# A fused attention and feed-forward kernel: its opening of 879 tasks in another order on all engines

## The chip, the cores and the metric

The kernel runs on one core of a Trainium2 chip. The metric is the device time of one execution in microseconds; the time before is the median of three runs. TensorE (PE) does matrix products, VectorE (DVE) and ScalarE (ACT) elementwise work and reductions, GpSimd (POOL) some elementwise work and DMA issues, and SyncE (SP) issues most DMAs. Each engine works through its own queue in order and waits for the others by semaphores.

## The reference

q, k and v have the shape (8 batches, 8 heads, 576 tokens, 64). The output of an attention with two parts goes through a gated feed-forward network:

```python
q_d, k_d, v_d = [t.reshape(B, H, 144, 4, D).mean(axis=3) for t in (q, k, v)]
out_d = softmax(q_d @ k_d.T / 8) @ v_d                       # coarse, per head
out_up = np.repeat(out_d, 4, axis=2)
mask = np.abs(pos[:, None] - pos[None, :]) < 4               # local, 7 keys a token
out_local = softmax(where(mask, q @ k.T / 8, -1e9)) @ v
x = (out_up + out_local).transpose(0, 2, 1, 3).reshape(4608, 512)
xn = x / sqrt(mean(x * x) + 1e-6) * rms_g
g, val = xn @ w_gate, xn @ w_val                             # 512 -> 1536
out = (g * sigmoid(g) * val) @ w_out                         # 1536 -> 512
```

## The kernel before

The 4608 tokens are cut into 18 chunks of 256. For each chunk the local attention gives x, x is normed and turned so that the features lie on the partitions, and the feed-forward part follows. x, the weights and the hidden values are each kept as a high and a low half (line 1051 and 1055 for x, 1435 and 1438 for the hidden values), and each product is done in three steps, high by high, high by low and low by high. `first` (line 1412) is a group of 12 products for one of 12 slices of the hidden layer, either gate or value; `second` (line 1453) is a group of six for the second layer.

The coarse attention (class `Coarse`) goes by batch and pair of heads: scores (line 589), maxima, powers, turns of the powers on TensorE (line 619), values (line 634). Its results go to DRAM and are read back by the chunks that add them. The local attention of most chunks (class `Attention`) runs on VectorE and ScalarE, with 7 keys for a token (lines 931, 935, 977, 984, 994). Chunks 0 and 1 (class `Early`, two units each) do it on TensorE instead (lines 1180, 1182 for scores, 1241 and 1252 for turns, 1272 for values, 1279 to add the coarse part, 1317 to turn x).

The weights arrive as 64-bit numbers in 20 pieces and are decoded (`decode`): a load on SP's queue, a scaling on ScalarE (line 267), the last bits on GpSimd (line 277), a join on VectorE (line 284), the high half on ScalarE (line 291) and the low half on VectorE, called a split (lines 296 and 298). Raw pieces share a few places, so a later load waits until an earlier piece has been split. The first four pieces are what the first `first` of chunk 0 needs.

All work from the start to the end of chunk 2's feed-forward part, with the local attention of chunks 2 and 3 and the coarse attention of batches 0 to 2, is written as 879 tasks. A task has an engine (or two to choose from: a negative number n in the order stands for task ~n on its second engine), a function that issues its instructions, tasks that must come before it, and buffers that it takes or uses. `ORDER` is a list of all tasks; `plan.run` issues them in that order. The order thus sets each engine's queue, and a wait for a semaphore is put in wherever a task needs another's result or buffer. The first `HELD` tasks are issued under a manual schedule, which keeps their order; those behind may be moved by the framework's scheduler, as may the rest of the kernel, which loops over chunks 3 to 17.

Task numbers that are named below: 0 and 37 load q and k of batch 0 (two halves), 1 and 38 v; 2 to 4 add up the first half, 5 and 42 reorder q; 549 loads the first weight piece, 555, 561, 567 the next three, 550 and 551 take the first one's last bits and scale it; 82 to 88 are the first scores of unit 0; 150 is the low half of chunk 0's second unit, 669 the first `first` of chunk 0, 733 and 734 its last `second` groups, 739 the first `first` of chunk 1, 451 the turn of chunk 2's x, 809 the first `first` of chunk 2, 874 its last `second`.

`run` before also keeps a small model of the engines: costs in microseconds per task, a delay from engine to engine, a DMA rate. From it `heat` (line 416) gets the idle time that TensorE would have ahead of a task, and fills 95% of that with products of a constant with zeros (line 457, called idle products here): 512 or fewer columns each, into a spare tile or into the tile that the next product will overwrite.

Of the kernel before, what the change touches and what calls it, by code (L numbers as in the profile page):

```python
# [19 lines left out]
P = 128  # L20
# [6 lines left out]
SP = S + 2 * HALO  # L27
# [22 lines left out]
HOP = {"PE": 0.25, "ACT": 0.2, "DVE": 0.15, "POOL": 0.2, "SP": 0.0}  # L50
WARM_AT = 6.5
COLD_UNTIL = 15.0
WARM_SHARE = 0.95
WARM_LEAST = 0.4
MB = 3.1
LAND = 2.0
# [44 lines left out]
]  # L101
HELD = 813


class Buf:
# [16 lines left out]
class Plan:  # L122
# [19 lines left out]
    def room(self, t):  # L142

        at, taken = 0.0, {}
        for b in t.allocs:
# [3 lines left out]
            if i >= len(order):  # L149
                return None  # L150
# [1564 lines left out]
```

## Time and profile before

| | us |
|---|---|
| median of 3 runs | 1088.38 (1087.9 to 1089.17) |
| the profiled execution | 1087.48 |
| its span, first to last instruction | 1085.7 |
| TensorE busy | 1062.6 (98%) |
| VectorE busy | 915.3 (84%) |
| ScalarE busy | 596.8 (55%) |
| GpSimd busy | 161.0 (15%) |

The execution is the span and what lies around it, 1.8 us. Busy time counts every instruction of an engine, the idle products too. The mean granted clock of TensorE over the span is 0.994 of full speed; 1 is 2.4 GHz and 0.5 is 1.2 GHz.

### The profile page before, as it was taken

Reading aid. Unit: us, or ns where it says so; the run is one execution under the profiler, and the core shown is the slowest. Engines: PE = TensorE matmul, PEld = TensorE weight load, DVE = VectorE, ACT = ScalarE, POOL = GpSimd, SP = SyncE. Lnnn points to the kernel's source line nnn. Section 1 sums busy time; section 2 is a strip of 40 time slices with the busy share of each in tenths; the row PEclk is TensorE's granted clock in tenths of the full one; section 3 lists DMA queues with packets and bytes.
Section 4 is the critical chain, followed back from the end, with each engine's and each line's share of the span. In section 5 each row is a group of like instructions: output and inputs, shape, how many; then the busy total and the mean of one; then the engine's idle time right before and its main releaser. Section 6 shows DMA issues by size and latency. Waiting matters only on the chain.

```text
span 1085.7 us, 21681 instructions
## 1 busy us (share of the span) xinstructions
PE 1062.6 (98%) x8013; PEld 964.6 (89%) x8013; DVE 915.3 (84%) x1556; ACT 596.8 (55%) x2029; POOL 161.0 (15%) x200
## 2 busy tenths in 40 slices
PE   7899999999999999999999999999999999999998
PEld 4668899998988999999999999999999989899997
DVE  7889899798969998989898989898989898985322
ACT  5775566647356556565555656464746464554111
POOL 5364454401110000000000000000000000000000
PEclk9899999999999999999999999999999999999999
DMA  9966557422644454444444443443222231300000
GB/s 292 326 168 190 143 126 167 99 78 73 149 95 108 99 127 104 123 83 113 91 103 109 102 112 95 116 98 85 72 76 72 74 87 56 104 16 20 1 21 20
DMA packets 78126, 113.83 MB, mean 105 GB/s; under 512 B 31966, under 2 KB 39334, under 8 KB 78020
## 3 DMA queue, kind: packets, MB, share of 16 engines
q1 hardware_dynamic: 48116, 88.11, 26.7%
q0 software_dynamic: 11680, 19.81, 11.9%
q10 hardware_dynamic: 18224, 4.53, 1.9%
q8 instruction: 63, 1.03, 0.4%
q14 instruction: 43, 0.35, 0.1%
HBM read 100.86 MB, written 11.53 MB: 104 GB/s over the span
## 4 chain that ended last, share of the span: by engine, by line
PE 74%; DVE 5%; ACT 2%; DMA 2%; issue 1%; POOL 1%; ACTq 0%; DVEq 0%; SPq 0%; POOLq 0%
PE ps_h L1412 45%; PE ps_o L1453 23%; PE ps_a L634 2%; ACT prod L977 1%; DVE x_t L994 1%; PE ps_a L589 1%; PE ps_a L619 1%; PE ps_a L1047 1%; DMA qk<-in_qk_sum_dram 1%; DVE prod L931 1%; DMA vs<-in_v_sum_dram 1%; DVE prod L984 1%; DVE sc L935 0%; DVE hs L1438 0%; DMA kv<-in_k_pad_dram 0%
## 5 line engine op out<-in xcount | busy, mean ns | idle before, releaser
L1412 PE MATMUL ps_h<-xh,w 128*128 128x256 f32 x3456 | 620.0, 279 | 0.0
L1412 PEld LDWEIGHTS ps_h<-xh,w 128*128 128x128 f32 x3456 | 532.3, 188 | 8.5 <-issue 4.5
L1412 PE MATMUL ps_h<-xl,w 128*128 128x256 f32 x1728 | 479.6, 278 | 0.0
L1453 PE MATMUL ps_o<-wo,hs 128*128 128x512 f32 x1296 | 328.8, 396 | 4.8 <-DVE hs L1438 3.7
L1412 PEld LDWEIGHTS ps_h<-xl,w 128*128 128x128 f32 x1728 | 324.9, 188 | 4.4 <-issue 0.6
L977 ACT ACTIVATE prod<-kv,sc 128x64 f32<-128x64 f32 x1024 | 263.2, 409 | 26.5 <-DVE sc L968 9.2
L1453 PEld LDWEIGHTS ps_o<-wo,hs 128*128 128x128 f32 x1296 | 231.8, 188 | 49.6 <-DVE hs L1438 6.3
L1435 ACT ACTIVATE hs<-sil 128x512 fp32r<-128x512 f32 x108 | 68.4, 633 | 173.9 <-DVE sil L1429 136.1
L931 DVE TENSOR_TENSOR prod<-q_t,kv 128x896 f32<-128x896 f32 x128 | 137.1, 1093 | 3.5 <-DMA q_t<-in_q_band_dram 2.9
L994 DVE TENSOR_REDUCE x_t<-prod 128x128 f32<-128x896 f32 x128 | 134.5, 1076 | 3.2 <-ACT prod L977 3.1
L935 DVE TENSOR_REDUCE sc<-prod 128x14 f32<-128x896 f32 x128 | 135.1, 1076 | 0.2
L1420 ACT ACTIVATE sil<-ps_h 128x512 f32<-128x512 f32 x108 | 64.5, 598 | 128.0 <-PE ps_h L1412 116.7
L1424 DVE SCALAR_TENSOR_TENSOR sil<-sil,ps_h 128x512 f32<-128x512 f32 x108 | 73.7, 683 | 52.7 <-ACT sil L1420 52.0
L984 DVE TENSOR_TENSOR prod<-sc,kv 128x384 f32<-128x384 f32 (+1 forms) x128 | 105.6, 862 | 0.2
L1429 DVE SCALAR_TENSOR_TENSOR sil<-sil,ps_h 128x512 f32<-128x512 f32 x108 | 74.0, 686 | 35.6 <-PE ps_h L1412 35.5
L1438 DVE TENSOR_TENSOR hs<-sil,hs 128x512 fp32r<-128x512 f32 x102 | 71.2, 698 | 19.4 <-ACT hs L1435 19.1
L369 POOL DMA_DIRECT2D qk<-in_qk_sum_dram x42 | 38.8, 923 | 231.6 <-DMA qk<-in_qk_sum_dram 187.9
L369 POOL DMA_DIRECT2D vs<-in_v_sum_dram x42 | 37.2, 886 | 235.1 <-DMA vs<-in_v_sum_dram 158.4
L609 ACT ACTIVATE a_g<-ps_a,m_g 72x144 f32<-72x144 f32 x128 | 46.6, 373 | 33.7 <-DVE m_g L604 21.3
L634 PEld LDWEIGHTS ps_a<-vs,a_g 72*72 72x72 f32 x512 | 39.1, 148 | 8.6 <-DVE a_g L709 3.6
L1017 ACT ACTIVATE up_t<-x_t 128x128 f32<-128x128 f32 x128 | 39.4, 308 | 10.7 <-DVE x_t L1007 8.8
L634 PE MATMUL ps_a<-vs,a_g 72*72 72x64 f32 x512 | 40.1, 232 | 4.2 <-DVE a_g L709 3.4
(155 smaller groups left out, 805.5 us busy)
## 6 DMA issues: line engine op xcount, KB each, us to landing
kv<-in_k_pad_dram SPq DMA_DIRECT2D x56, 320.0 KB
kv<-in_v_pad_dram SPq DMA_DIRECT2D x56, 320.0 KB
qk<-in_qk_sum_dram POOLq DMA_DIRECT2D x42, 288.0 KB, 4.6
out_dram<-o_sb SPq DMA_DIRECT2D x92, 72.0 KB
vs<-in_v_sum_dram POOLq DMA_DIRECT2D x42, 144.0 KB, 3.8
q_t<-in_q_band_dram SPq DMA_DIRECT2D x150, 36.0 KB
w<-in_w_gate_dram SPq DMA_DIRECT2D x8, 512.0 KB
w<-in_w_val_dram SPq DMA_DIRECT2D x8, 512.0 KB
```

Source lines behind the costliest of these rows:

```text
L369: nc.gpsimd.dma_start(out=t, in_=(qk_sum, v_sum)[i][self.b, j, :, self.half], accum_op=ALU.add)
L634: in_line(lambda: nc.tensor.matmul(out=op[:, par, c], lhsT=at[:, kc, c * HALF:(c + 1) * HALF], rhs=self.sums.vs[:, 2 * (self.hp % 2) + par ...
L931: nc.vector.tensor_tensor(out=pr, in0=bcast(q[:, s0:s0 + 2], 2, NO), in1=window(k, s0), op=ALU.mult)
L935: nc.vector.tensor_reduce(out=self.sc[:, j, par, s0:s0 + 2], in_=self.pr[i], axis=AX.X, op=ALU.add,)
L977: nc.scalar.activation(out=self.pr[i][:, o, s], in_=self.v[j, par][:, s0 + s + o], func=AF.Copy, scale=p[:, s, o:o + 1],)
L984: (nc.vector if engine == "DVE" else nc.gpsimd).tensor_tensor(out=self.pr[i][:, a:b], in0=bcast(p[:, :, a:b].rearrange("p s o -> p o s"), ...
L994: nc.vector.tensor_reduce(out=self.x[j][:, s0:s0 + 2, par], in_=pr.rearrange("p o s d -> p s d o"), axis=AX.X, op=ALU.add,)
L1412: self.last = nc.tensor.matmul(out=p[n][:, i], lhsT=wi[:, k], rhs=xi[:, k], start=(m == 0), stop=(m == 3 * KT - 1),).ins
L1424: nc.vector.scalar_tensor_tensor(out=self.sil[n], in0=self.sil[n], scalar=1.0, in1=self.g[n], op0=ALU.add, op1=ALU.mult,)
L1429: nc.vector.scalar_tensor_tensor(out=self.sil[n], in0=self.sil[n], scalar=0.5, in1=self.v[n], op0=ALU.mult, op1=ALU.mult,)
L1438: low["last"] = (nc.gpsimd if engine == "POOL" else nc.vector).tensor_tensor(out=self.hs[n][:, 1], in0=self.sil[n], in1=self.hs[n][:, 0], ...
L1453: in_line(lambda: nc.tensor.matmul(out=self.o[j], lhsT=lhs[:, j * P:(j + 1) * P], rhs=rhs, start=(f == 0 and m == 0), stop=(f == NF - 1 an ...
```

## The change

The 879 tasks stand in another order. The first 850 of them, in place of 813, keep it; the last 29 may be moved by the scheduler. The small model of the engines is gone: `run` only checks that what a task needs has been issued. Idle products are now written down by task, in `IDLE`: 26 of 512 columns, ahead of six tasks (46 and 82, 86, 113, 158, 174: scores and a turn), in place of 135. Some tasks change engines: VectorE has 305 of the tasks in place of 310, ScalarE 224 in place of 222, GpSimd 90 in place of 87. The tasks themselves, and the code behind the opening, are the same. The diff, with all but the first rows of the two orders left out:

```diff
-HOP = {"PE": 0.25, "ACT": 0.2, "DVE": 0.15, "POOL": 0.2, "SP": 0.0}
-WARM_AT = 6.5
-COLD_UNTIL = 15.0
-WARM_SHARE = 0.95
-WARM_LEAST = 0.4
 MB = 3.1
-LAND = 2.0
 ISSUE = 0.75
 ORDER = [
-    151, 0, 37, 182, 76, 75, 77, 78, 549, 5, 2, 3, 4, 1, 153, 82, -185, 9, 83, 84, 42, 39, 555, 11, 10, 12, 40,
-    14, 41, 13, 17, 550, 38, 85, 18, 15, 551, 90, 23, 19, -17, 92, 110, 552, 152, 91, 567, -7, 79, 86, -8, 88,
...
+    77, 549, 551, 75, 0, 2, 79, 5, 3, 4, 110, 37, 82, 182, 76, -185, 78, 9, 10, 11, 83, 1, 555, 84, 85, 90, 42,
+    39, 550, 91, 12, 552, -7, 86, 87, 14, -8, 13, 92, 17, 18, 151, 88, 23, 89, 24, 15, 573, 93, 25, 26, 94, 28,
...
 ]
-HELD = 813
+HELD = 850
+IDLE = {46: 2, 82: 10, 86: 6, 113: 4, 158: 1, 174: 3}
...
     def run(self, order):
 
-        free = self.free
         for n in order:
             t = self.tasks[max(n, ~n)]
-            e, cost, _ = t.options[n < 0]
-            at = self.room(t)
-            assert at is not None and all(a.end is not None for a in (*t.after, *t.with_)), n
-            known = max(free[e], at)
-            s = max([known, t.not_before, free["DMA"] - 3.0 if t.dma else 0.0] + [a.end for a in t.after] + [a.start + 0.01 for a in t.with_])
-            t.start = self.now = s
-            self.idle, self.gap = (s - max(known, WARM_AT), s - max(free[e], WARM_AT)) if e == "PE" else (0.0, 0.0)
-            free[e] = s + cost
...
-            t.engine = e
+            assert self.room(t) and all(a.done for a in (*t.after, *t.with_)), n
+            t.done = True
             for b in t.allocs:
                 self.order[b.res].append(b)
-            t.fn(e) if len(t.options) > 1 else t.fn()
+            self.now = t.n
+            t.engine = t.options[n < 0][0]
+            t.fn(t.engine) if len(t.options) > 1 else t.fn()
...
     def heat(out, fresh=True):
 
-        n = plan.idle
+        n = IDLE.get(plan.now, 0)
+        if not n:
+            return
         if spare["open"] and made:
             if "tile" not in spare:
                 spare["tile"] = ps_o.tile([P, DM], FP32, name="ps_o")
-            out, fresh, n = spare["tile"], True, plan.gap
-        n, plan.idle, plan.gap = n * WARM_SHARE, 0.0, 0.0
+            out, fresh = spare["tile"], True
...
-        rate = 1200 if plan.now < COLD_UNTIL else 2400
-        for _ in range(int(n * rate / cols) if n > WARM_LEAST and made else 0):
+        for _ in range(n * 4 * P // cols):
```

## Rows read from the trace of the kernel before

**Rows 1.** Windows by stage: us, busy us (instructions), granted clock, DMA share, GB/s.

```profile
6.60:76.40 69.80, 61.63 (x373) 40.38 (x374) 61.28 (x111) 50.37 (x139) 37.01 (x40) 0.93 0.87 277
76.40:166.20 89.80, 89.80 (x694) 79.53 (x693) 83.87 (x127) 53.94 (x129) 46.15 (x56) 1.00 0.61 153
166.20:258.20 92.00, 91.86 (x661) 84.33 (x660) 77.92 (x133) 50.59 (x185) 24.59 (x37) 1.00 0.44 98
258.20:400.00 141.80, 139.23 (x1105) 127.62 (x1104) 128.08 (x221) 84.97 (x329) 17.31 (x20) 1.00 0.49 113
400.00:800.00 400.00, 400.00 (x3147) 372.80 (x3147) 364.83 (x639) 228.89 (x833) 31.77 (x37) 1.00 0.42 102
```

The engines in each row are PE, PE's weight loads, DVE, ACT and POOL.

**Rows 2.** Windows of line 457 alone, the idle products: PE, PE's weight loads.

```profile
0.00:76.40 76.40, 20.53 (x72) 7.38 (x72) 0.93 0.85 274
...
98.00:128.00 30.00, 10.79 (x58) 5.64 (x58) 1.00 0.74 192
...
258.00:400.00 142.00, 0.71 (x5) 0.55 (x5) 1.00 0.49 113
```

**Rows 3.** Timeline of PE: start us, us, line, out<-in, count.

```profile
76.42 0.47 PE L1412 MATMUL ps_h<-xh,w 128*128 128x256 f32 x1
...
98.26 4.94 PE L457 MATMUL ps_o<-zero_sb,one_sb 128*128 128x512 bf16 x22
102.84 1.74 PE L1453 MATMUL ps_o<-wo,hs 128*128 128x512 f32 x6
```

**Rows 4.** Timelines of DVE, ACT and POOL, 6 to 13 us: [idle before <-releaser].

```profile
6.66 0.76 DVE L425 TENSOR_TENSOR qk<-w 128x576 f32<-128x576 f32 x1 [0.79 <-DMA w<-in_qk_sum_dram]
...
6.66 1.99 ACT L419 COPY hs<-w 128x1024 f32<-128x1024 f32 x1 [3.45 <-DMA w<-in_qk_sum_dram]
9.73 2.00 ACT L419 COPY hs<-w 128x1024 f32<-128x1024 f32 x1 [1.08 <-DMA w<-in_qk_sum_dram]
...
12.82 1.10 POOL L277 TENSOR_SCALAR w<-w 128x1024 uint32<-128x1024 uint16 x1 [3.70 <-DMA w<-in_w_val_dram]
```

**Rows 5.** Groups of DVE's instructions, 6.6 to 76.4 us: busy us, mean ns, idle before.

```profile
L284 DVE SCALAR_TENSOR_TENSOR w<-w 128x1024 uint32<-128x1024 uint32 x8 | 10.0, 1249 | 0.5 <-ACT w L267 0.5
L1195 DVE TENSOR_REDUCE m_e<-ps_h 128x2 f32<-128x272 f32 x16 | 6.8, 430 | 3.5 <-PE ps_h L1182 3.5
...
L433 DVE TENSOR_TENSOR vs<-vs,w 72x512 f32<-72x512 f32 x3 | 2.9, 962 | 0.9 <-POOL vs L433 0.8
L1165 DVE TENSOR_TENSOR kv<-kv,side_sb 64x512 f32<-64x512 f32 x2 | 2.3, 1136 | 0.0
...
L709 DVE COPY a_g<-ps_a 72x288 f32<-72x288 f32 x2 | 0.9, 438 | 0.1
L709 DVE COPY prod<-ps_a 128x512 f32<-128x512 f32 x1 | 0.7, 692 | 0.1
...
L1307 DVE TENSOR_SCALAR x_t<-x_t,rinv 128x512 f32<-128x512 f32 x1 | 0.5, 486 | 0.0
```

**Rows 6.** Windows around PE's longest wait, columns as in the first group.

```profile
32.00:36.00 4.00, 0.60 (x6) 0.60 (x7) 3.97 (x6) 3.13 (x8) 1.49 (x3) 0.95 1.00 342
36.00:42.00 6.00, 6.00 (x34) 4.63 (x33) 5.44 (x8) 3.98 (x9) 2.98 (x3) 0.50 0.82 239
```

**Rows 7.** Timeline of PE around the same wait.

```profile
30.53 0.76 PE L1182 MATMUL ps_h<-w,hs 64*128 64x136 f32 x4
...
35.40 1.11 PE L634 MATMUL ps_a<-vs,a_g 72*72 72x64 f32 x8 [3.44 <-DVE a_g L709]
...
36.67 1.27 PE L1182 MATMUL ps_h<-w,hs 64*128 64x136 f32 x4
```

**Rows 8.** Windows by stage, behind the opening, columns as in the first group.

```profile
320.00:340.00 20.00, 18.34 (x144) 17.02 (x143) 18.84 (x27) 17.54 (x68) 4.20 (x5) 1.00 0.58 121
340.00:360.00 20.00, 19.52 (x140) 17.58 (x139) 20.00 (x29) 5.51 (x20) 0.00 (x0) 1.00 0.29 82
```

More of the change, by code (lines that the diff above doesn't have):

```diff
@@ L112, with __init__ @@
 class Task:
-    def __init__(self, n, options, fn, due, after, with_, allocs, uses, not_before, dma, lag):
-        self.n, self.options, self.fn, self.due = n, options, fn, due
-        self.after, self.with_, self.allocs = after, with_, allocs
-        self.not_before, self.dma, self.lag = not_before, dma, lag
-        self.start = self.end = None
+    def __init__(self, n, options, fn, after, with_, allocs, uses, dma, lag, not_before):
+        self.n, self.options, self.fn, self.after, self.with_, self.allocs = n, options, fn, after, with_, allocs
+        self.dma, self.lag, self.not_before, self.done = dma, lag, not_before, False
         for b in (*allocs, *uses):
@@ L125, in __init__ @@
     def __init__(self, bufs):
-        self.tasks, self.bufs, self.idle, self.now = [], bufs, 0.0, 0.0
-        self.free = {e: 0.0 for e in ("PE", "ACT", "DVE", "POOL", "SP", "DMA")}
+        self.tasks, self.bufs, self.now = [], bufs, None
         self.order = {r: [] for r in bufs}
@@ L135, in add @@
         t = Task(
-            len(self.tasks), options, fn, due, [a for a in after if a], [a for a in with_ if a],
-            [*allocs, *[Buf("hw") for _ in range(hw)], *[Buf("sw") for _ in range(sw)]], list(uses), not_before, dma, lag,
+            len(self.tasks), options, fn, [a for a in after if a], [a for a in with_ if a],
+            [*allocs, *[Buf("hw") for _ in range(hw)], *[Buf("sw") for _ in range(sw)]], list(uses), dma, lag, not_before,
         )
@@ L142, in room @@
     def room(self, t):
-        at, taken = 0.0, {}
+        taken = {}
         for b in t.allocs:
@@ L148, in room @@
             taken[b.res] = taken.get(b.res, 0) + 1
-            if i >= len(order):
-                return None
-            if i >= 0:
-                for u in order[i].users:
-                    if u.end is None:
-                        return None
-                    at = max(at, u.end)
-        return at
+            if i >= len(order) or i >= 0 and not all(u.done for u in order[i].users if u is not t):
+                return False
+        return True
     def run(self, order):
-        free = self.free
         for n in order:
             t = self.tasks[max(n, ~n)]
-            e, cost, _ = t.options[n < 0]
-            at = self.room(t)
-            assert at is not None and all(a.end is not None for a in (*t.after, *t.with_)), n
-            known = max(free[e], at)
-            s = max([known, t.not_before, free["DMA"] - 3.0 if t.dma else 0.0] + [a.end for a in t.after] + [a.start + 0.01 for a in t.with_])
-            t.start = self.now = s
-            self.idle, self.gap = (s - max(known, WARM_AT), s - max(free[e], WARM_AT)) if e == "PE" else (0.0, 0.0)
-            free[e] = s + cost
-            if t.dma:
-                free["DMA"] = max(free["DMA"], s + cost) + t.dma
-                t.end = free["DMA"] + LAND
-            else:
-                t.end = s + cost + (t.lag or HOP[e])
-            t.engine = e
+            assert self.room(t) and all(a.done for a in (*t.after, *t.with_)), n
+            t.done = True
             for b in t.allocs:
                 self.order[b.res].append(b)
-            t.fn(e) if len(t.options) > 1 else t.fn()
+            self.now = t.n
+            t.engine = t.options[n < 0][0]
+            t.fn(t.engine) if len(t.options) > 1 else t.fn()
 @with_exitstack
@@ L1594, in attn_moe_kernel @@
     plan.run(ORDER[HELD:])
+    plan.now = None
     att, late, behind = atts[FIRST], [], None
```

78 rows, old and new, of the table ORDER are left out of this document.

## The prediction

> **What bounds the kernel now.** I read the busy time by stage first. From 76.4 us on TensorE is busy in every stage, fully so from 400 to 800 us, where VectorE has 364.83 of 400 us [rows 1]. What TensorE gets done earlier in the opening therefore reaches the end of the run, as long as VectorE keeps up. The opening's loss is hidden in the word busy: the idle products of line 457 are counted as TensorE work. Windows of that line alone show 20.53 us of them before 76.4 us and 10.79 us between 98 and 128 us [rows 2]. They are waits written as work. TensorE's timeline shows both kinds of place: the first product of the feed-forward part at 76.42 us, and 22 idle products from 98.26 to 102.84 us while the first second-layer product waits for its hidden values [rows 3]. Ahead of the first feed-forward product VectorE has 61.28 us of work in 69.80 us, and between 76.4 and 166.2 us 83.87 in 89.80 [rows 1]. So VectorE sets the pace of the opening up to about 166 us, with 8.5 and 5.9 us of idle time of its own, and TensorE sets it afterwards (VectorE 77.92 of 92.00 us, TensorE 91.86).
>
> Three sums decide the change: what stands in VectorE's queue ahead of the first feed-forward product, how VectorE's and TensorE's queues keep pace behind it, and what is left of TensorE's idle time between 258 and 400 us.
>
> **Part 1: up to the first feed-forward product.** Its last condition is the low half of the first chunk's x (the split of unit 1, task 150) and the four decoded pieces of W1 (tasks 554, 560, 566, 572). I list VectorE's tasks ahead of task 150 in both orders: 95 before, 86 after, the same but for twelve that leave and three that enter. Leaving: four joins of weight bits that are needed only later (606, 600, 594, 624), 4 x 1.25; one placing of edges that goes to GpSimd (81), 1.14; two copies of 72x288 (16, 32), 2 x 0.44; one copy of 128x512 (134), 0.69; one norm (143), 0.49; two maxima (190, 192), 2 x 0.43; one tiny scaling that I leave out. That is 9.1 us by the means of these lines [rows 5]. Entering: a 128x512 copy (100), 0.69; an addition of v (45), 0.96; a copy of an edge (105), which I bound by the 72x288 copy at 0.44. That is 2.1 us. VectorE's queue ahead of task 150 gets 7.0 us shorter. TensorE's own queue ahead of task 669 holds the same 50 tasks.
>
> Against this stands the load order. SP's queue begins with 0, 37, 549 before, and with 549, 0, 37 after. The three land at 6.66, 9.73 and 12.82 us: the first addition and the first reordering copy wait for the first, the second copy for the second, the last-bits step for the third [rows 4]. So a weight piece takes 12.82 - 9.73 = 3.1 us of the queue, and in the new order the q and k sums land 3.1 us later. VectorE's first addition moves from 6.66 to about 9.8 us, and until then VectorE has only the masks to build. ScalarE's first task becomes the scaling of that piece, which is over before the q sums land, so it costs nothing there.
>
> VectorE's remaining idle time of 8.5 us is what no row of before prices in the new order. Below, it falls to about 4 us when the first two units' scores, softmax and turns follow each other as closely as the order puts them; above, it grows by 3 us because TensorE, without idle products to bring it to the higher clock, does its small products later. I take it as unchanged. Part 1 then gives 7.0 - 3.1 = 3.9 us: task 669 at about 72.5 us.
>
> The idle products themselves cost nothing before 72 us in either order, and so give nothing: before, they lie in time in which TensorE waits for VectorE and ScalarE (the wait is still 3.44 us long at 35.40 us [rows 7]); after, 26 of them remain, 10 ahead of the first score and 6 ahead of the third, both of which wait for q anyway.
>
> **Part 2: behind it, to the end of the opening.** All six places that keep idle products (tasks 46, 82, 86, 113, 158, 174) come before task 669. From there to task 874 the new order has none, where before has 10.79 us of them [rows 2] and 0.14 us of idle time [rows 1]. Real TensorE work is the same. How long TensorE waits now follows from VectorE. From task 669 to the second-layer product 733, which needs the last decoded pieces of W2, TensorE's new queue has 31 groups of 12 first-layer products, 10 groups of second-layer products and 20 small ones: 69.8 us by their durations in the trace. VectorE's queue from behind task 150 to the split 662 has 91 tasks, among them 13 joins, 13 splits, 17 score steps of the local attention and 16 gates, products and low halves: 70.7 us. So both engines are full. With VectorE's busy share of the like stretch before, 83.87 / 89.80 = 93% [rows 1], its 70.7 us take 75.7, and TensorE waits 5.9 us. A second point is the turn of chunk 2's x (task 451): TensorE 110.9 us, VectorE 148 tasks and 110.8 us, 118.6 at 93%, so 7.7 us. Bounds: 1 us if VectorE is never idle, 10.9 us (nothing gained) if the waits return in full. I take 7. Part 2 gives 10.9 - 7 = 3.9 us.
>
> **Part 3: behind the opening.** Between 258.2 and 400 us TensorE is idle for 141.80 - 139.23 = 2.6 us and runs 0.71 us of idle products [rows 1, 2]; VectorE is busy for 38.84 of the 40 us from 320 to 360 [rows 8]. Before, tasks from the 814th on could slip behind other work; now only the last 29 can, and all products of the third batch's coarse attention stand ahead of task 874, so its results, which chunk 4 adds, are ready earlier. The gain lies between 0 and 3.3 us; I take 1.1.
>
> The sum is 3.9 + 3.9 + 1.1 = 8.9 us. The profiled execution took 1087.48 us (span 1085.7 and 1.8 around it) and would take 1078.6. The median of the three runs lies 0.9 above it, so I predict 1088.38 - 8.9 = 1079.5 us. The bounds are 0.9 to 8.4 for part 1, 0 to 9.9 for part 2 and 0 to 3.3 for part 3. Their ends seldom meet; the half-widths of 3.8, 5 and 1.7, added as squares, give 6.5, and the forecast's own range is 1073 to 1086.
>
> **Rivals.**
>
> *The clock falls: slower.* TensorE's granted clock went to 0.50 (the 1.2 GHz level) from 36 to 42 us, right behind its idle stretch of 3.44 us, in a window of 32 to 36 us in which it was busy for 0.60 [rows 6, 7]. At that level four score products took 1.27 us instead of 0.76 [rows 7], 1.67 times. With 26 idle products in place of 72 ahead of task 669, TensorE has longer gaps. Its real work between 6.6 and 76.4 us is 61.63 - 20.53 = 41.1 us [rows 1, 2]; at the lower level throughout that would be 68.6, start at 11.8 us (q lands at 9.8, its reordering takes 2.0 [rows 4]) and end no earlier than 80 us, with some of today's waits at about 85. Part 1 turns from 3.9 gained to 8.6 lost, and the run ends at 1092. TensorE's free time in the new opening is 72.5 - 11.8 - 41.1 - 5.4 = 14 us, with 26 idle products at 0.21 (22 took 4.6 us [rows 3]); it covers some 21 us of work done at the lower level, and beyond that each further microsecond of such work costs 0.67. Against it: the mean grant from 6.6 to 76.4 us is 0.93, so only 14% of it ran at the lower level, although TensorE was idle for 8.2 us there [rows 1]. The Trainium skill, "TensorE: Matmul & The Clock Gate", section "Part 1: The HAM clock gate", speaks for this rival: it says that the lower level is the default, and that activity lifts it. By that rule alone the new opening would run low more often; the trace agrees so far as it shows one fall after one idle stretch. Chance 0.11.
>
> *VectorE takes it back.* It is busy for 97% from 320 to 360 us [rows 8]. If chunk 4's attention does not start earlier with TensorE, TensorE waits there, and the gains of parts 2 and 3 go; part 1's 3.9 stays, since VectorE itself is ahead by it: 1084.5. Against it: VectorE is idle for 14.1 us between 166.2 and 258.2 [rows 1], so it has room to start earlier. Chance 0.14.
>
> *No change.* SP's queue now has unit 2's values (task 152) behind two weight pieces (585 and 597), whose loads must wait until VectorE has split the pieces that stand in the same place. Its values product stands in TensorE's queue ahead of the turns of the first chunk's x. If these values land 4 us late, part 1 is gone; and if the waits of part 2 return in full, what is left is part 3: 1087.5. Chance 0.08.
>
> The forecast has the remaining 0.67. A measurement of this kernel tells a change from none at about 0.2%, 2.2 us. Faster: 0.66 of the forecast's 0.67 and 0.12 of VectorE's 0.14, 0.78. Slower: 0.10 of the clock's 0.11 and nothing else. Same: the rest, 0.12. The range of 8 in 10 reaches from a little below the forecast's own to the no-change case: 1070 to 1088.
>
> **What would show it.** Step 1: task 669, the first product of line 1412, at 70 to 75 us, the first addition of line 425 at about 9.8 us. Step 2: no idle products behind it, 4 to 9 us of TensorE idle time up to the last second-layer product of chunk 2, most of it put down to VectorE's hidden values or weight splits. Step 3: less than 2 us of idle time in the 140 us after. The prediction is wrong if the first product of line 1412 comes after 78 us with the granted clock at 0.5 for much of the time before (the clock), or if the opening is over 7 us earlier but the idle time behind it grows (VectorE).

## The result and the profile after

The changed kernel takes 1099.98 us (median of 5 runs, 1094.27 to 1104.45), the kernel before 1087.90 beside it: a ratio of 1.0102 [1.0067, 1.0138]. Faster by 9 us was forecast; it is slower by 12, beyond the range. Both parts of the loss stand in the windows by stage. Below are the rows of after that answer to [rows 1], columns as there; a line of after has a number 24 lower than before (1388 for 1412, 1429 for 1453, 433 for 457, 401 for 425).

```profile
6.60:76.40 69.80, 66.02 (x314) 46.19 (x311) 49.01 (x101) 43.54 (x127) 28.95 (x38) 0.66 0.75 225
76.40:166.20 89.80, 88.02 (x688) 80.23 (x686) 82.39 (x131) 58.22 (x139) 50.60 (x59) 0.98 0.70 187
166.20:258.20 92.00, 88.06 (x643) 78.50 (x642) 74.81 (x126) 51.32 (x189) 29.89 (x37) 0.98 0.52 110
258.20:400.00 141.80, 132.80 (x997) 122.26 (x996) 131.22 (x224) 82.61 (x309) 13.62 (x14) 0.96 0.42 99
400.00:800.00 400.00, 400.00 (x3133) 372.47 (x3132) 363.61 (x628) 230.27 (x844) 33.41 (x39) 1.00 0.43 102
```

Ahead of 76.4 us TensorE looks busier than before (66.02 against 61.63), although its 26 idle products take 11.40 us in place of the 20.53 of [rows 2]; the granted clock has gone from 0.93 to 0.66. VectorE has 12 us less work behind it (49.01 against 61.28). From 258 to 400 us TensorE is idle for 9.0 us where it was for 2.6. Two closer windows of after:

```profile
25.00:73.00 48.00, 46.75 (x218) 35.23 (x218) 32.18 (x66) 29.13 (x82) 18.60 (x22) 0.50 0.64 185
...
255.00:290.00 35.00, 27.49 (x174) 24.25 (x173) 33.18 (x58) 19.21 (x73) 5.82 (x5) 0.82 0.43 111
```

From 25 to 73 us TensorE is busy for 46.75 of 48 us, all of it at 0.50, the 1.2 GHz level. It is idle for only 1.25 us there, and the other engines wait for it: ahead of 76.4 us VectorE waits 8.1 us for score products, in place of the 3.5 us of [rows 5]. From 255 to 290 us it is VectorE that is full and TensorE that waits, and the clock falls again. The first product of line 1388 (task 669) comes at 79.12 us, before at 76.42 [rows 3]:

```profile
79.12 0.68 PE L1388 MATMUL ps_h<-xh,w 128*128 128x256 f32 x1
```

To set runs side by side I count TensorE's work done by a given time: every product that has ended, at the median length that its line has in the kernel before at the upper level (0.113 us for line 1412, 0.230 for line 1453, and so on), idle products at nothing. "Lead" is that sum minus the same of the kernel before. The changed kernel is behind by 2.9 us at 80 us, ahead by 3.2 at 140, even at 250 (0.2), behind by 13.6 at 300 and by 10.8 at 400. So the new order wins 6 us between 80 and 140 us, gives back 3 of them by 250 and loses 14 between 250 and 300. In all runs that keep the new order up to task 669, another 2 to 4 us are lost behind 400 us, where TensorE is fully busy until 800 (e4 is ahead by 1.7 at 400 us, and its profiled execution ends 1.1 behind that of before); in e9, with the old order, the lead stays. No run asks why. The expectations' "third chunk" is chunk 3, the last whose local attention belongs to the opening.

| run | median us | ratio to before | task 669 at | turn of chunk 3's x at | lead at 140 | 250 | 300 | 400 |
|---|---|---|---|---|---|---|---|---|
| before | 1087.9 | 1 | 76.4 | 254.0 | 0 | 0 | 0 | 0 |
| after | 1099.98 | 1.0102 | 79.1 | 271.0 | 3.2 | 0.2 | -13.6 | -10.8 |
| e1, root on GpSimd | 1097.04 | 1.0077 | 78.9 | 268.8 | 3.1 | -1.0 | -10.5 | -8.2 |
| e2, 813 held | 1102.10 | 1.0132 | 71.9 | 272.9 | 7.6 | 1.2 | -14.7 | -14.4 |
| e3, tail of before | 1097.44 | 1.0095 | 79.0 | 267.5 | 2.8 | -10.3 | -10.0 | -10.6 |
| e4, more idle products | 1090.53 | 1.0023 | 72.9 | 262.5 | 9.7 | 4.8 | -0.3 | 1.7 |
| e5, before without any | 1095.08 | 1.0049 | 88.1 | 263.8 | -10.0 | -9.3 | -8.6 | -8.6 |
| e6, e4 with 41 tasks moved | 1090.52 | 1.0017 | 71.3 | 251.4 | 9.9 | 0.7 | 0.0 | 2.4 |
| e7, e4, scores held back | 1097.56 | 1.0092 | 77.9 | 256.2 | 4.7 | 1.1 | -3.5 | -13.3 |
| e8, e4, loads as before | 1090.75 | 1.0009 | 73.0 | 264.1 | 8.4 | 2.9 | -4.1 | -2.3 |
| e9, before, head's idle products only | 1079.61 | 0.9922 | 78.4 | 252.1 | 3.3 | 2.1 | 2.5 | 2.8 |
| e10, before, VectorE more | 1107.29 | 1.0179 | 74.7 | 272.5 | 1.8 | -17.9 | -17.1 | -18.6 |
| e11, e6, some scores held back | 1091.12 | 1.0039 | 71.2 | 244.9 | 12.0 | 3.2 | 4.5 | 1.4 |
| e12, e4, chunk 3's scores cheap | 1088.80 | 1.0004 | 74.4 | 265.6 | 8.2 | 2.2 | -4.0 | -1.8 |
| e14, e4, chunk 4's scores cheap | 1081.80 | 0.9943 | 71.4 | 251.1 | 10.1 | 7.2 | 5.7 | 9.1 |
| e15, e9 with more in the head | 1084.18 | 0.9969 | 75.1 | 247.2 | 6.7 | 6.9 | 7.1 | 7.5 |

The medians are of all runs of a kernel; times of tasks and leads are those of its one profiled execution, which can lie away from the median. A single execution also has its luck: e4, e6, e7, e11, e12 and e14 have the same list up to task 669 and the same idle products, and it comes at 71.2 to 77.9 us in them. There is no e13.

### The profile page after: what moved, and what is told of

The parts are those of the page before. It is cut to its first block, busy times and chain, and to the rows that moved or that the text cites. A ratio compares the mean times of both kernels' runs of the same rounds, so it can differ in the third digit from the quotient of the medians.

```text
span 1098.8 us, 21470 instructions
## 1 busy us (share of the span) xinstructions
PE 1067.3 (97%) x7904; PEld 972.0 (88%) x7904; DVE 910.8 (83%) x1559; ACT 597.1 (54%) x2031; POOL 158.3 (14%) x192
## 4 chain that ended last, share of the span: by engine, by line
PE 73%; DVE 6%; ACT 2%; DMA 2%; issue 1%; SPq 1%; POOL 0%; ACTq 0%; DVEq 0%; POOLq 0%
PE ps_h L1388 45%; PE ps_o L1429 22%; PE ps_a L610 2%; DVE x_t L970 1%; ACT prod L953 1%; DVE prod L907 1%; PE ps_a L565 1%; PE ps_a L1023 1%; PE ps_a L595 1%; DMA qk<-in_qk_sum_dram 1%; DVE sc L911 1%; DVE prod L960 1%; DVE sil L1405 1%; DMA q_t<-in_q_band_dram 0%; DVE sil L1400 0%
## 5 line engine op out<-in xcount | busy, mean ns | idle before, releaser
L1414 DVE TENSOR_TENSOR hs<-sil,hs 128x512 fp32r<-128x512 f32 x98 | 68.3, 697 | 21.1 <-ACT hs L1411 21.0
L610 PEld LDWEIGHTS ps_a<-vs,a_g 72*72 72x72 f32 x512 | 41.4, 157 | 6.2 <-ACT a_g L683 2.1
L993 ACT ACTIVATE up_t<-x_t 128x128 f32<-128x128 f32 x128 | 39.1, 306 | 11.7 <-DVE x_t L983 10.1
```

What stands on the lines that cost most here:

```text
L610: in_line(lambda: nc.tensor.matmul(out=op[:, par, c], lhsT=at[:, kc, c * HALF:(c + 1) * HALF], rhs=self.sums.vs[:, 2 * (self.hp % 2) + par ...
L1414: low["last"] = (nc.gpsimd if engine == "POOL" else nc.vector).tensor_tensor(out=self.hs[n][:, 1], in0=self.sil[n], in1=self.hs[n][:, 0], ...
```

## The experiments

### The clock ahead of the first feed-forward product: e4, e5

e4 leaves the new order alone and lists more idle products, nearly all at tasks between 20 and 72 us. (The expectation says 66; the list adds up to 70 of 512 columns, which makes 77 instructions.)

```diff
-IDLE = {46: 2, 82: 10, 86: 6, 113: 4, 158: 1, 174: 3}
+IDLE = {82: 10, 86: 6, 113: 4, 20: 8, 46: 4, 117: 6, 34: 4, 106: 4, 158: 4, 137: 4, 174: 5, 178: 8, 189: 3}
```

> The changed kernel with 66 idle products instead of 26, all ahead of the first feed-forward product, most of them at the values, scores and turns between 23 and 72 us. Clock theory: the granted clock stays at the upper level for most of the first 76 us, the first feed-forward product comes at 72 to 75 us instead of 79, and the run takes 1085 us or less. Late-chain theory: the first product comes earlier too, but TensorE still runs out of work near 258 us and waits for the third chunk's x, so the run takes 1094 to 1100 us.

The same window of e4 as above, with the clock at 0.94:

```profile
25.00:73.00 48.00, 47.62 (x313) 31.09 (x311) 34.70 (x77) 34.06 (x94) 22.83 (x24) 0.94 0.73 220
```

Task 669 comes at 72.9 us, TensorE is ahead by 9.7 us at 140 us, and the run takes 1090.53 us: 9.5 us of the 12 come back, to 1.0023 [1.0004, 1.0042]. Neither theory had it alone. The first product comes when the clock theory said, but the lead is gone again at 300 us, and the kernel is not faster than before.

The number of idle products alone does not decide when the clock rises. e2 (below) has the list and the 26 idle products of after up to task 669; its clock rose at 53.6 us, in after at 72.8, and task 669 came at 71.9 us instead of 79.1. Two rows of e2, and one of e7, which has the list and idle products of e4 up to task 669:

```profile
25.00:53.00 28.00, 28.00 (x139) 21.79 (x140) 19.63 (x45) 16.98 (x56) 12.24 (x14) 0.50 0.47 154
53.60:71.90 18.30, 17.67 (x126) 12.43 (x125) 15.21 (x34) 17.88 (x43) 9.19 (x10) 1.00 1.03 293
```

```profile
36.00:77.90 41.90, 41.81 (x232) 27.51 (x231) 27.05 (x57) 26.84 (x65) 14.73 (x14) 0.80 0.62 176
```

In e7 the clock was at 0.50 from 35.6 to 52.6 us, TensorE was busy without a gap behind 36 us, 10.22 us of it with idle products, and task 669 came at 77.9 us. There the idle products stood in the way of real ones.

e5 takes the idle products out of the kernel before.

```diff
-        n, plan.idle, plan.gap = n * WARM_SHARE, 0.0, 0.0
+        n, plan.idle, plan.gap = 0.0, 0.0, 0.0
```

> The kernel before, its old order kept, with all 135 idle products left out. Clock theory: the granted clock is at 0.5 for much of the first 76 us, the first feed-forward product comes at 80 to 85 us instead of 76.4, and the run takes 1092 to 1100 us. The view of the prediction (idle products lie in waits and give nothing, those behind 76 us hold 10.8 us that could be used): the first product stays at 76 to 77 us and the run takes 1083 to 1089 us.

Task 669 comes at 88.1 us, 11.7 later and beyond the expected 80 to 85; the lead is -10 at 140 us and stays near -9; the run is slower, 1.0049 [1.0026, 1.0072]. So the old order's idle products too carry the clock, and the clock theory holds. The row for the first stage seems to deny it, since its clock is 1.00. The groups of products say otherwise: five rows follow: the window, the same group of products in e5 (10 to 76 us) and in the kernel before (43 to 62 us, clock 1.00), with busy us and mean ns, and two rows of e5's timeline.

```profile
6.60:76.40 69.80, 61.86 (x273) 44.37 (x272) 56.86 (x104) 45.11 (x126) 32.16 (x36) 1.00 0.82 269
```

```profile
L1182 PE MATMUL ps_h<-w,hs 64*128 64x136 f32 x54 | 17.2, 470 | 0.0
...
L1182 PE MATMUL ps_h<-w,hs 64*128 64x136 f32 x24 | 4.6, 309 | 0.0
```

```profile
93.00 0.63 PE L1412 MATMUL ps_h<-xh,w 128*128 128x256 f32 x2
...
95.01 0.40 PE L1412 MATMUL ps_h<-xh,w 128*128 128x256 f32 x2
```

A score product of line 1182 takes 470 ns there, as it does in after at a granted 0.50 (471 ns), in place of 309, and two of line 1412 take 0.63 us until 94.7 us and 0.40 behind it. The trace has its first record of the clock at 94.6 us, and the page fills the time before it with 1.00. This run was at the lower level from its start. The Trainium skill, "TensorE: Matmul & The Clock Gate", section "Part 1: The HAM clock gate", says that the lower level is the default and that activity lifts it; e5 agrees: its clock rose for the first time 6.5 us after the first feed-forward product. The same section warns that records of the clock can be unreliable; here the products' lengths show where.

### The loss between 250 and 300 us: e1, e2, e3, e6

The waits of TensorE in after, 240 to 300 us (us in total, times, longest):

```profile
PE ps_o L1429 <- ACT hs L1411: 3.0, 1, 3.0
PE ps_h L1388 <- ACT xh L1027: 2.9, 1, 2.9
PE ps_o L1429 <- DVE hs L1414: 1.3, 1, 1.3
PE ps_a L610 <- DVE o_g L628: 1.2, 1, 1.2
```

They are for chunk 2's hidden values and then for chunk 3's x. VectorE's timeline shows why both are late. The root of chunk 3's norm (task 540, moved from GpSimd to VectorE, `-541` in the new list) is nine small instructions, each of which needs the one before. Between them stand lines 907 and 911, the score steps of chunk 4's local attention. These belong to the code behind the opening, and the scheduler places them.

```profile
260.20 0.16 DVE L709 SCALAR_TENSOR_TENSOR newton<-rinv 128x8 f32<-128x8 f32 x1
260.29 1.09 DVE L907 TENSOR_TENSOR prod<-q_t,kv 128x896 f32<-128x896 f32 x1
261.30 1.08 DVE L911 TENSOR_REDUCE sc<-prod 128x14 f32<-128x896 f32 x1
262.30 0.15 DVE L710 TENSOR_TENSOR newton<-newton,rms 128x8 f32<-128x8 f32 x1
262.37 0.68 DVE L1405 SCALAR_TENSOR_TENSOR sil<-sil,ps_h 128x512 f32<-128x512 f32 x1
262.97 1.08 DVE L911 TENSOR_REDUCE sc<-prod 128x14 f32<-128x896 f32 x1
263.96 2.05 DVE L907 TENSOR_TENSOR prod<-q_t,kv 128x896 f32<-128x896 f32 x1
265.94 1.23 DVE L711 SCALAR_TENSOR_TENSOR rinv<-newton,rinv 128x8 f32<-128x8 f32 x1
...
269.61 1.28 DVE L1010 TENSOR_TENSOR x_t<-x_t,rinv 128x512 f32<-128x512 f32 x2
```

From the first step of the norm (253.25 us) to its last product (269.61) it takes 16.4 us; in the kernel before, 241.1 to 250.4 us, 9.3. The first remedies were read from this: the root back to GpSimd (e1), the old number of fixed tasks (e2), the old order for the last part (e3).

```diff
-    ... 539, -541, 338, 541, 545 ...
+    ... 539, 540, 338, 541, 545 ...
```

> The changed kernel with one task moved: the root of the third chunk's norm (task 540) goes back from VectorE to GpSimd. Late-chain theory (TensorE runs out of work at 261 us because the third chunk's x comes 20 us later than before; its root took 9.3 us on VectorE between chunk 4's score steps, 3.7 us on GpSimd before): the first norm moves from 269.6 to about 263 us, TensorE waits 5 to 7 us less between 255 and 290 us, the run takes about 1094 us. Clock theory (the loss is the lower clock from 25 to 73 us): no change, about 1100 us.

1097.04 us, 1.0077 [1.0051, 1.0102]: 3 us come back, half of what was expected, and the interval overlaps that of after. The norm comes at 265.0 us, not 263, and the wait for chunk 2's hidden values grows to 4.4 us.

```diff
-HELD = 850
+HELD = 813
```

> The changed kernel with 813 tasks fixed instead of 850, so that 66 are left to the scheduler as before. If fixing 37 more tasks is what costs: TensorE's waits between 255 and 290 us go and the run is near 1088 us. Late-chain theory: the steps that make the third chunk's x late (tasks 500 to 528) stand ahead of the 813th, so at most 3 us come back, 1097 to 1100 us. Clock theory: 1100 us.

1102.10 us: fixing 37 more tasks is not the cause. This run shows something else. By chance of the clock its task 669 came at 71.9 us (see e4) and its lead at 140 us is 7.6, and it still is 14.7 behind at 300 us. The clock ahead of 76 us can't be all.

```diff
-plan.run(the new list), HELD = 850
+plan.run(the first 724 of the new list, then the other 155 as in the old one), HELD = 813
```

> The changed kernel's first 724 tasks, idle products included, then the remaining 155 in the order and on the engines of the kernel before (seven of them moved where a buffer demands it), 813 fixed. Late-chain theory: the third chunk's x is ready near 258 us, TensorE's waits between 255 and 290 us fall from 10 us to under 3, and the run takes 1085 to 1090 us although the first 76 us run at the lower clock as in the changed kernel. Clock theory: the first 76 us are unchanged, so the run stays at 1096 to 1100 us.

1097.44 us. The lead at 250 us is -10.3 already: where the two orders meet TensorE waits for VectorE's gates (8.5 us between 220 and 240 us). From 250 to 300 us nothing is lost. The old tail doesn't have the late loss, but it does not fit behind the new head, so the run says nothing about the price.

e6 goes on from e4. The root is on GpSimd, and 41 tasks behind the 600th are moved, chunk 3's late steps forward, steps of the third batch's coarse attention back.

```diff
-    ... 344, -541, 349 and others at their places in the new list
+    ... 540; 504, 505, 506, 538, 546 and others 5 to 38 places earlier; 349, 313 some 40 places later
```

> The changed kernel with the 66 idle products of the run before and 41 tasks behind the 600th moved within their engines' queues: the root of the third chunk's norm on GpSimd, the chunk's late value products, its mean and turns some places further ahead, steps of the third batch's coarse attention further back. If the clock and the late third chunk are the two causes, both are met: the first feed-forward product at 73 us, the third chunk's turn by 258 us, TensorE's waits between 166 and 300 us under 5 us instead of 8.7, and the run at 1077 to 1084 us. If the late chunk is not a cause: 1088 to 1092 us, as with the idle products alone.

1090.52 us, as e4. Chunk 3's x is turned 11 us earlier than in e4 (251.4 us), and nothing is won: the lead falls from 9.9 us at 140 to 0.7 at 250, earlier than in e4. TensorE waits for chunk 2's hidden values instead (VectorE, 3.4 us at 244.5), which now stand behind the same score steps of chunk 4. So the theory that chunk 3's place alone makes the loss fails.

### Is VectorE short of time, or are chunk 4's steps in the wrong place? e10, e12, e7, e11, e14

e10 adds VectorE work to the kernel before.

```diff
-            nc.vector.tensor_tensor(out=pr, in0=bcast(q[:, s0:s0 + 2], 2, NO), ...)
+            for _ in range(17 if self.c == FIRST and i == 6 else 1):
+                nc.vector.tensor_tensor(out=pr, in0=bcast(q[:, s0:s0 + 2], 2, NO), ...)
```

> The kernel before with one score step of the third chunk's local attention (task 478, 1.08 us on VectorE) done 17 times over, with the same result: 16 to 17 us more of VectorE work ahead of the third chunk's x, in the old order. If VectorE's place in the third chunk's chain is what the late loss hangs on: the third chunk's turn comes 8 to 14 us later, TensorE waits between 200 and 290 us where it waited for nothing before, and the run takes 1096 to 1104 us. If VectorE had room to make it up (14 us of idle time from 166 to 258 us): 1088 to 1092 us.

```profile
PE ps_h L1413 <- DVE sil L1430: 17.8, 1, 17.8
```

1107.29 us, 1.0179 [1.0161, 1.0197], some 19.5 us more for 16 to 17 us of work, and nearly all of it in one wait. VectorE's queue goes in order, and TensorE's next group needed a gate from behind the repeated step. This shows the price of a block at one place, not that VectorE lacks time.

e12 takes work away from VectorE (all of chunk 3's score steps at an eighth of their width).

```diff
+            d = slice(0, 8 if self.c == FIRST else D)
-                out=pr, in0=..., in1=window(k, s0), op=ALU.mult)
+                out=pr[:, :, :, d], in0=...[:, :, :, d], in1=window(k, s0)[:, :, :, d], op=ALU.mult)
```

> The changed kernel with the 66 idle products, and the third chunk's local scores taken over 8 of the 64 values of each head instead of all (the score products and their sums; everything else is computed as before): about 13 to 15 us less VectorE work between 144 and 206 us. If VectorE's lateness is what takes the gain of the new order back by 270 us: the third chunk's norm comes at 250 us or before instead of 261, TensorE waits under 4 us between 166 and 300 us instead of 8.7, keeps the 9 us that it is ahead at 140 us, and the run takes 1077 to 1083 us. If the order of the last third is to blame whatever VectorE has to do: 1087 to 1091 us.

1088.80 us, 1.0004 [0.9985, 1.0024], within the spread of e4. The row is that of the stage from 166 to 258 us; behind it the place where the time went.

```profile
166.20:258.20 92.00, 86.14 (x624) 77.95 (x623) 60.16 (x123) 46.72 (x170) 27.53 (x34) 0.96 0.51 111
```

```profile
196.60 0.69 DVE L1034 TENSOR_TENSOR xl<-ps_a,xh 128x512 fp32r<-128x512 f32 x1 [3.84 <-ACT xh L1030]
197.21 0.43 DVE L914 TENSOR_REDUCE sc<-prod 128x14 f32<-128x112 f32 x2
```

VectorE is busy for 60.16 of 92 us and idle for the rest. Chunk 3's last score sums stand in its queue behind the low half of chunk 2's x, wait with it, and are done at 198 us as in e4. VectorE is not short of time there: it spends it waiting, and cheaper steps only make the wait longer. Behind 240 us it is different. Two rows for 240 to 360 us, before and e4, and the first of chunk 4's score steps in before and in after:

```profile
240.00:360.00 120.00, 117.43 (x898) 106.46 (x897) 105.08 (x179) 64.49 (x243) 15.75 (x27) 1.00 0.45 107
...
240.00:360.00 120.00, 113.79 (x866) 103.78 (x865) 115.03 (x193) 63.24 (x233) 11.12 (x12) 0.99 0.43 104
```

```profile
223.58 1.08 DVE L931 TENSOR_TENSOR prod<-q_t,kv 128x896 f32<-128x896 f32 x1
...
244.66 1.09 DVE L907 TENSOR_TENSOR prod<-q_t,kv 128x896 f32<-128x896 f32 x1
```

In e4 VectorE is busy for 115.03 of 120 us there, before for 105.08. The kernel before has done most of chunk 4's score steps by 240 us; after starts them at 244.7 us, e4 at 238.0. They fall into the stretch in which VectorE is nearly full.

e7 and e11 put chunk 4's score steps behind chunk 3's norm, all of them (e7, in e4's order with the root on GpSimd) or from the fourth on (e11, in e6's order).

```diff
+            with tc.issue_after(normed[FIRST]) if self.c == FIRST + 1 else nullcontext():
                 nc.vector.tensor_tensor(out=pr, in0=bcast(q[:, s0:s0 + 2], 2, NO), ...)
```

> The changed kernel with the 66 idle products, the root on GpSimd, and chunk 4's score products on VectorE issued behind the third chunk's norm. If these score steps, which the scheduler puts between the third chunk's last steps, make the chunk late: the norm comes at 250 to 254 us instead of 261, TensorE's waits from 240 to 285 us fall to 3 us or less, and the run takes 1081 to 1086 us. If VectorE has no time left for them later, the wait only moves to chunk 4 (300 to 380 us) and the run stays at 1088 to 1093 us.

> The mended order with its 66 idle products, and chunk 4's score products from the fourth on issued behind the third chunk's norm; the first three may go ahead of it. If these score steps between the third chunk's last steps are what takes the gain back: the norm comes at 246 us or before instead of 249.8, TensorE's wait at 244 us (3.4 us) falls under 1.5 us, and the run takes 1083 to 1087 us. If VectorE's time is short as a whole: the wait comes back at chunk 4's x (325 to 345 us) and the run stays at 1089 to 1095 us.

e7 takes 1097.56 us, e11 1091.12. Chunk 3's x is turned earlier than in the orders that they start from (256.2 against 262.5 us, 244.9 against 251.4), and then TensorE waits for chunk 4's x, which is turned at 332.8 us in e7, in place of e4's 320.8, and at 318.9 in e11, no earlier than e6's 318.5. The waits of e7 from 300 to 400 us:

```profile
PE ps_a L1023 <- DVE x_t L1010: 5.2, 1, 5.2
PE ps_h L1388 <- ACT xh L1027: 3.6, 1, 3.6
```

That is the second expectation of each run, which says that VectorE has no time left for these steps later (e7's time lies above its range). They can't simply be put off.

e14 makes chunk 4's score steps cheap and leaves everything where it is in e4. It has the same edit as e12, with `FIRST + 1` in place of `FIRST`.

> The changed kernel with the 66 idle products, and chunk 4's local scores (not the third chunk's) taken over 8 of the 64 values of each head, everything else computed as before: about 14 us less VectorE work in steps that the scheduler puts between the third chunk's last steps from 240 us on. If these steps are what takes the early gain back (cheaper scores of the third chunk itself did not help): the norm comes at 252 us or before instead of 261, TensorE waits 4 us or less between 240 and 300 us, is still 5 us or more ahead of the kernel before at 300 us, and the run takes 1079 to 1085 us. If the third chunk is late by its place in the queues alone: the norm stays at 258 us or later and the run at 1087 to 1091 us.

1081.80 us, 0.9943 [0.9921, 0.9965]: 8.7 us less than e4, for about as much VectorE work left out as in e12, where it gave nothing. From 240 to 290 us (first e4, then e14, in a fence each):

```profile
240.00:290.00 50.00, 43.79 (x340) 39.11 (x338) 49.53 (x84) 29.52 (x113) 5.95 (x6) 0.97 0.42 106
```

```profile
240.00:290.00 50.00, 47.60 (x375) 43.13 (x375) 46.99 (x94) 31.56 (x122) 7.31 (x7) 1.00 0.52 130
```

And the norm of chunk 3 in e14, first step and last product, with the root on VectorE as in after:

```profile
245.38 0.16 DVE L698 TENSOR_SCALAR rms<-ps_a 128x8 f32<-128x8 f32 x1
...
250.34 1.22 DVE L1013 TENSOR_TENSOR x_t<-x_t,rinv 128x512 f32<-128x512 f32 x2
```

It takes 5.0 us in place of 14.6 in e4 (246.58 to 261.17 us), TensorE is idle for 2.4 us in place of 6.2, its clock does not fall, and most of the lead is kept. So the late loss is made by chunk 4's score steps, which stand between the opening's last steps on VectorE. Whether it is their place there or the time that they take from a full VectorE is not separated: e14 changes both, and e7 and e11, which change the place alone, win nothing. e14 leaves out work and is no candidate; it prices the steps where they stand.

### What the idle products behind 76 us are worth: e9, e15, and e8

e9 is the second part of the prediction done alone, in the old order.

```diff
-... if e == "PE" else (0.0, 0.0)
+... if e == "PE" and self.tasks[670].start is None else (0.0, 0.0)
```

> The kernel before, its old order and the idle products ahead of the first feed-forward products kept, all idle products behind them left out. By the second part of the prediction (10.9 us of idle products behind 76 us, of which waits take back about 7): TensorE has done about 4 us more real work at 140 us than in the kernel before, and the run takes 1083 to 1086 us. Clock theory: the waits in their place bring the granted clock down for one or two stretches of 3.4 to 6.8 us before 166 us, each costing half its length, and the run is within 3 us of the kernel before.

1079.61 us, 0.9922 [0.9903, 0.9941], below what either theory expected and the fastest of all that compute everything. It is the median of four runs, and the profiled one is the slowest of them, 1084.19 us, 3.3 less than the profiled execution of before; the other three took 1078.61 to 1079.94. In that trace task 669 comes 2 us later than before, and between 80 and 140 us TensorE gains 5.3 us of real work. Its row for the stage:

```profile
76.40:166.20 89.80, 88.30 (x673) 79.22 (x672) 87.61 (x135) 59.39 (x154) 49.41 (x62) 0.98 0.65 160
```

TensorE waits for 1.5 us where 10.8 us of idle products stood, and VectorE does 87.61 us in place of the 83.87 of [rows 1]. The clock falls once, for 3.4 us.

e15 adds to e9 more idle products in the head.

```diff
-WARM_SHARE = 0.95, WARM_LEAST = 0.4
+WARM_SHARE = 1.15, WARM_LEAST = 0.2
```

> The kernel before without the idle products behind the first feed-forward products, and with more of them ahead of it (1.15 instead of 0.95 of each expected wait, from 0.2 us on instead of 0.4). Clock theory: fewer stretches at the lower clock ahead of the first feed-forward product than the 17 us of the run with the head's idle products unchanged, the first product at 74 to 76 us, and the run takes 1076 to 1080 us. If the idle products get in the way of real ones: the first product at 78 us or later and the run at 1081 to 1085 us.

1084.18 us, 0.9969 [0.9945, 0.9992], with runs from 1079.25 to 1089.30. The profiled execution has what was expected of it (task 669 at 75.1 us, 1079.25 us), the median has not. That more idle products in the head help the old order is not shown; its interval lies above that of e9, which had four runs in another session.

e8 is e4 with the old head of SP's queue (0, 37, then 549).

> The changed kernel with the 66 idle products and the head of SP's queue as before: the q and k pieces first, the weight piece third. By the load term of the prediction (3.1 us): the first addition at 6.7 instead of 9.1 us, the first feed-forward product at 70 us instead of 72.9. If that time is lost in the waits behind it: the first product at 72 to 74 us. Either way the end of the run moves by 3 us at most from 1090.5 us, since the third chunk's x still comes late.

1090.75 us, 1.0009 [0.9994, 1.0024]. The first addition comes at 6.5 us, and task 669 at 73.0 all the same, so the 2.6 us are lost in the waits behind it.

## Why the prediction was wrong

**Part 1** failed at one sentence: "The idle products themselves cost nothing before 72 us in either order, and so give nothing". They carry the clock. Task 669 was to come at 72.5 us and came at 79.1; with 44 more units of idle products and the same order it came at 72.9 (e4). A second term was off as well: VectorE's idle time, taken as unchanged at 8.5 us, became 69.80 - 49.01 = 20.8. The clock is only a part of that, since in e4, with the clock at 0.90, it is still 18.15 us up to task 669. That e4 meets the sum's 72.5 is therefore luck. Its row:

```profile
6.60:72.90 66.30, 63.79 (x380) 39.14 (x378) 48.15 (x103) 45.14 (x130) 33.34 (x40) 0.90 0.82 247
```

VectorE does 48.15 us of work there, 13.1 less than the 61.28 of [rows 1], where the sum had 7.0 less, and is idle for 18.15 us, where the sum had 8.5 + 3.1. The two errors nearly cancel. The load term of 3.1 us was 2.5 in place (first addition at 9.13 us, expected at 9.8), and nothing at task 669 (e8, one execution).

**The clock rival** was described rightly and given 0.11. Its time for task 669 (85 us) was too late, its time for the run (1092) too early, since it priced no second loss. The argument against it was the mean grant of 0.93 in [rows 1], "only 14% of it ran at the lower level". That number was too good. Before 15.1 us the trace of before has no record, and its four score products at 8.70 us take 1.27 us, the length that [rows 7] shows at 0.50:

```profile
8.70 1.27 PE L1182 MATMUL ps_h<-w,hs 64*128 64x136 f32 x4 [2.39 <-ACT hs L419]
```

And the grant was good because of the 20.53 us of idle products of [rows 2], so it couldn't speak for an order without most of them. The trace also has a second fall, from 62.9 to 66.3 us, that the rival's text leaves out.

**Part 2** held up to task 451, where its sums ended, and failed behind it. Foreseen were 3.9 us gained between task 669 and the end of the opening; the lead rises by 6.1 us from 80 to 140 us in after, by 7.2 in e4, by 5.3 in e9. The turn of chunk 2's x (task 451) comes 4.4 us earlier in after (196.3 against 200.7), 117.2 us behind task 669 in place of 124.3; TensorE waits for 2.4 us on the way, not for the 7 of the sum. As foreseen there are no idle products behind 76 us. But the part was to reach to task 874, and the last second-layer product of chunk 2 ends at 271.1 us in after and at 258.2 before: what was gained is lost within the opening.

**Part 3**, and the end of part 2 with it, failed, and that is the second large error. Part 3 foresaw 0 to 3.3 us gained behind 258 us, and less than 2 us of TensorE idle time; after has 9.0 us, and loses 14 us of lead between 250 and 300. The pace of VectorE was worked out at two points, tasks 733 and 451, and not at the third, the turn of chunk 3's x. Three things there weren't priced: chunk 3's maxima come at 205.0 us instead of 184.2, behind chunk 2's x in VectorE's queue; the root is on VectorE, which the list of engine changes showed; and chunk 4's score steps, which run from 224 to 247 us before, while TensorE still has other work, start at 244.7 in after and fall between the last steps of chunks 2 and 3. e14 puts 8.7 us on the last of these, beside the 9.5 us that e4's clock gives back.

**The VectorE rival** (1084.5, chance 0.14) had the place nearly right, TensorE's lead lost to VectorE behind the opening, and its condition, that chunk 4's attention does not start earlier, was met: it starts 21 us later. Its argument against itself, VectorE's idle time between 166.2 and 258.2 us, did not help, since the order leaves VectorE waiting there (e12) and nearly full behind it. It was wrong in size: it left part 1's gain in place, 1084.5 us. The no-change rival named pieces 585 and 597 on SP's queue; no wait of TensorE in the trace points to them.

With both causes taken away (e4's idle products, e14's cheap steps) the new order gives 1081.8 us, 2.3 from the 1079.5 predicted. That doesn't make the sum right, since e14 leaves out VectorE work (894.4 us of it in the whole run, in e4 905.1). What stays open is a new order that does so with all of its work: e6, e7 and e11 moved the wait and didn't remove it. A list in which chunk 4's score steps stand by hand wasn't tried.

## What to carry to other kernels

An idle product did two things here: it held a place and it held the clock. Before one is taken out, look whether the stretch ahead of real work would still keep TensorE at the upper level, and keep those in the head. The cheapest gain here was to take out those that stand where real work was waiting (e9). An agreement with a sum is worth little until its terms are checked one by one (e4). When an order is judged by the pace of its queues, go on to the last consumer in it, and look at what the scheduler may put between the steps of a short chain: here each small step then waited for a long one.

## What the runs showed of the hardware

TensorE at 0.50 stayed there for 48 us while busy for 46.75 of them, on score, turn and value products (471 and 328 ns each for lines 1158 and 610). The rise came at 72.8 us, behind three idle products and eight turns; in e2, with the same list, it came at 53.6 us. So a busy share near 1 stood beside either level: [rows 1] has 400.00 of 400 us at 1.00.

A granted clock of 1.00 ahead of a trace's first record of it is no measurement. In e5 that record came at 94.6 us, and the lengths of the products (470 ns against 309) tell what the clock was before it. The mean clock of a run then misleads too: of e5's ten runs the seven slower ones (1094.68 to 1097.01 us) show 0.996 to 0.998, the three faster ones (1089.37 to 1089.84) 0.989. Only one of the slower ones has a trace.

The times of the five runs of after go with their mean clock, nearly in order: 1094.27 us at 0.980, 1096.78 at 0.975, 1100.61 at 0.970, 1099.98 at 0.969, 1104.45 at 0.968. Their spread is 10 us, where the kernel before has 3.4 in the five runs beside them (and 9.1 in 19 runs of a later session).

In the rows of the root above, a score product takes 2.05 us in place of 1.08, and the step of line 711 behind it 1.23 in place of 0.16. Both lie in the time from 263.79 to 267.15 us in which GpSimd made the low halves of two hidden values (line 1414), so VectorE may be slowed while GpSimd works beside it. In e1 the first product of chunk 3's norm takes 3.58 us from 265.03 us on, beside 2.81 us of the same low halves on GpSimd (from 265.24), where e4 has 0.68. No run here tests it.
